# Attention and mixer on one core: loads of pairs 1 and 3, bursts of pairs 4 to 7, and new unit orders

## The chip, the cores and the metric

The kernel runs on one core of a Trainium2 chip. The metric is device time in microseconds of one execution; the time given is the median of several runs. Engines are TensorE (PE), VectorE (DVE), ScalarE (ACT), GpSimd (POOL) and SyncE (SP). SP, ACT and POOL issue DMAs; POOL's are software DMAs, which can also turn fp32 into bf16.

## The reference

```python
batch, n_heads, seq, head_dim = (4, 8, 768, 64); n_sink, window = (4, 128)
scores = scale * q @ k.T                      # scale = 1/sqrt(64)
keep = (key < n_sink) | (0 <= query - key < window)
a = softmax(where(keep, scores, -1e9)); attn = a @ v
x = attn as [4, 768, 512]                     # heads side by side
h = relu(x.T @ w_tok1) @ w_tok2               # w_tok1 768x256, w_tok2 256x768
u = x + h.T
out = u + relu(u @ w_ch1) @ w_ch2             # w_ch1 512x1536, w_ch2 1536x512
```

All inputs and the output are fp32.

## The kernel before

The 32 heads are worked on as 16 pairs, four (NHP) for each batch; pair p is batch p // 4. For a pair, q and k must come to lie with the head's 64 elements on the partitions (`qT`, `kT`); then come the scores of the window and of the sinks, exp, the mask, and the product with v (`v_aug`, with a column of ones for the sum of the weights).

**Loads.** Pairs 0 to 3: SP loads q and k as fp32 into a place each of `early` (`load_raw`), and an engine casts them to `q_bf`, `k_bf` (`cast`). Pairs 4 to 7: POOL's software DMA loads and casts; PE turns them. Pairs 8 to 15 (BY_DMA = 8): POOL's DMA loads and casts, and a DMA transpose of SP turns them. The v of all pairs and the four weights (T w_tok1, A w_tok2, C w_ch1 and D w_ch2 in quarters) are loaded by POOL. The four sink rows of v of batch 0's heads are loaded by SP in four DMAs into `v_sink_f`, and POOL casts that tile to `v_sink`. A cast waits for the landing, a turn for the cast.

**Turning by PE.** For pairs 0 to 4, `turn(p, n)` turns q (n = 0) or k (n = 1) into two of the four small PSUM banks (`mx`), 128x384 each. For pairs 5 to 7, `transposed(p)` turns q and k into one of the two double banks (`sc`), which two evictions of 128x768 read; since scores will later be written there by small tiles and then read whole, the bank's unwritten columns are set to zero (`cleared`, a memset of DVE).

**Scores.** `scores(p, g)` has three groups g of keys for a pair. `by_halves` makes four matmuls of 128 keys for a group (three in another shape for the last), `by_eighths` sixteen of 32 keys that leave out more of what the mask drops. Pairs 4 to 7 do group 0 by halves and the others by eighths; pairs 8 to 15 do all by eighths. `score_sinks(p)` makes the scores of the sinks of two pairs.

**Values.** `pv(p, half)` multiplies the weights with v and the sinks' weights with `v_sink`, in full tiles of 128 rows. Pairs 4 to 7 had another form: `sink_values(p)`, eight matmuls in small tiles within a burst, and two `values(p, i)`.

**Order.** A class `Plan` runs once, while the program is built. It holds a cost for each operation (`Op`) and a time for each landing (`landed(at)`), and gives each operation other than PE's to an engine and a place in its order. PE's order is given by tables: FIRST_BATCH for batch 0 (q0 and k0 turn pair 0's q and k; m01 adds the mask of pair 0's group 1 and s01 makes its scores; x1 makes the sinks' scores of pairs 0 and 1; o10 is `pv(1, 0)`; h0 the first step of the mixer over tokens; u00 and y01 the second step; t00 a transpose of u), MERGED for all that follows (t: units of `attention_and_tokens`; c: units of the mixer over channels, `mix_channels`), and LOADS for POOL's loads. A `burst` is one PE unit made of pieces that use small tiles (64 rows or 32 columns); PE changes between these and full tiles at its ends. `attention_and_tokens` makes two bursts for each of the pairs 4 to 7 and three for two pairs from 8 on.

Every engine runs its instructions in the order so fixed.

Of the kernel before, what the change touches and what calls it, by code (L numbers as in the profile page):

```python
# [9 lines left out]
FP32 = mybir.dt.float32  # L10
BF16 = mybir.dt.bfloat16
# [5 lines left out]
def kernel(  # L17
# [167 lines left out]
    raws = {p: load_raw(p) for p in range(2)}  # L185
    vs = {}


    ones = singles.tile([P, 4 * P], BF16)
    in_order(nc.vector.memset(ones, 1.0))  # L190

# [45 lines left out]
    v_sink_f = singles.tile([P, NHP, 2, D1], FP32)  # L237
    in_order(nc.vector.memset(v_sink_f, 0.0))
    for n in range(4):
        i, odd = n // 2, n % 2  # L240
        rows = slice(D * i + ODD * odd, D * i + ODD * odd + n_sink)
# [4 lines left out]
        in_order(nc.vector.memset(v_sink_f[rows, odd::2, i, D:D1], 1.0))  # L246
    raws.update({p: load_raw(p) for p in range(2, NHP)})
# [212 lines left out]
    def prepare(p):  # L460
# [4 lines left out]
        parts = 2 if p <= NHP else 1  # L465
# [55 lines left out]
    def transposed(p):  # L521

        def run():
            ps = turned_bank(p)
            for n in range(2):
                turn_rows(p, n, [ps[:, x, n] for x in range(2)])
                tiles["ps_" + "qk"[n], p] = ps[:, :, n].rearrange("d x j p -> d x p j")

        then = [*done["qT", p], *done["kT", p]]
        then.append(cleared(p, then))  # L530
        return piece(
            350, run, [done["q_bf", p], done["k_bf", p]], {"sc": [then]}, then, [("tq", p), ("tk", p)],
        )
# [37 lines left out]
    def scores(p, g):  # L571
# [4 lines left out]
        eighths = p >= BY_DMA or p >= NHP and g > 0  # L576
# [361 lines left out]
    def attention_and_tokens():  # L938
# [13 lines left out]
        for p in range(first, BY_DMA):  # L952
            b, hp = pairs[p]
            pieces = []
            prepare(p + 1)
            if p + 1 < BY_DMA:
                pieces.append(transposed(p + 1))
# [7 lines left out]
            if hp == NHP - 1:  # L965
                pieces += turned
            if hp % 2 == 0:
                pieces.append(score_sinks(p + 1))
            units.append(burst(*pieces))
            units[-1].then.append(sink_rows(p))  # L970
            if hp == 2:
                turned = tokens(b, 0)

        for p in range(BY_DMA, last, 2):
            b, hp = pairs[p]
            prepare(p + 1)
            units.append(burst(scores(p, 0), scores(p, 1)))
            units[-1].then.append(sink_rows(p))
            units += [pv(p - 1, half) for half in range(2)]
            turned = [] if hp else tokens(b - 1, 1)  # L980
            if p + 2 <= last:
                prepare(p + 2)
            units.append(burst(scores(p, 2), scores(p + 1, 0), score_sinks(p + 1), *turned))
            units[-1].then.append(sink_rows(p + 1))
            if hp == 0:
                parts.append(units)
                units = []
            units += [pv(p, half) for half in range(2)]
            if hp == 2:
                assert not tokens(b, 0)  # L990
            units.append(burst(scores(p + 1, 1), scores(p + 1, 2)))
# [318 lines left out]
    def cast(p, n, at):  # L1310
        cost = {"POOL": 850.0} if p == NHP - 1 else {"DVE": 570.0} if p or n else {"ACT": 850.0}
        return Op(cost, lambda e: copy(e, bf_tile(p, n), raws[p][n]), [landed(at)])

    for p, at in enumerate(((3900.0, 5300.0), (7500.0, 8600.0), (11300.0, 12500.0), (13500.0, 14700.0))):
        for n, name in enumerate(("q_bf", "k_bf")):
            queue((name, p), cast(p, n, at[n]))
    v_sink = Op({"POOL": 650.0}, lambda e: copy(e, v_sink0, v_sink_f), [landed(9000.0)])
# [3 lines left out]
    done["v", 0] = landed(12600.0)  # L1321
# [78 lines left out]
```

## Time and profile before

| | us |
|---|---|
| median of 3 runs | 195.93 (195.38 to 196.03) |
| profiled execution, time | 196.29 |
| profiled execution, span of the core | 194.5 |
| PE busy in the span | 186.1 (96%) |
| DVE, ACT, POOL busy | 135.0, 106.0, 60.2 |

The span runs from the first to the last recorded instruction; 1.8 us of the profiled execution lie around it. Busy time is that in which an instruction of the engine runs; the granted clock of PE is 1.0 throughout.

### The profile page before, as it was taken

How to read it: one execution, taken by the hardware profiler on the slowest of the kernel's cores; microseconds unless marked ns; L12 is line 12 of the kernel's file. 1: busy time of each engine (PE TensorE's matmuls, PEld its weight loads, DVE VectorE, ACT ScalarE, POOL GpSimd, SP SyncE). 2: the span in 40 equal slices, each digit the busy share in tenths (PEclk: the TensorE clock that was granted, in tenths of full speed). 3: DMA queues.
4: the chain of work that ended last, by engine and by line, in shares of the span. 5: the costliest groups of instructions: out<-in, count | busy, mean ns of one | idle time of the engine just before them, and what ended most of it. 6: DMA issues, size and time to landing. Idle time of an engine off the chain costs nothing.

```text
span 194.5 us, 5919 instructions
## 1 busy us (share of the span) xinstructions
PE 186.1 (96%) x2548; PEld 130.4 (67%) x2555; DVE 135.0 (69%) x299; ACT 106.0 (54%) x183; POOL 60.2 (31%) x78
## 2 busy tenths in 40 slices
PE   6896999999999999999999999999999999999992
PEld 1344797566664565566767887667668886667891
DVE  4678677887977657777789788786597762067671
ACT  4699747888864414777753536786461005764100
POOL 7379662509984851536900000000000000000000
PEclk9999999999999999999999999999999999999999
DMA  5999999999999999999999954500000717000036
GB/s 188 279 289 178 202 205 189 191 192 169 158 137 143 127 217 131 223 206 126 139 147 143 144 111 136 219 3 0 3 0 2 149 54 285 3 0 0 0 113 216
DMA packets 82139, 26.35 MB, mean 135 GB/s; under 512 B 69952, under 2 KB 79296, under 8 KB 82112
## 3 DMA queue, kind: packets, MB, share of 16 engines
q0 software_dynamic: 56864, 11.80, 75.7%
q1 hardware_dynamic: 25248, 14.17, 34.3%
q8 instruction: 20, 0.33, 0.7%
q14 instruction: 7, 0.06, 0.1%
HBM read 26.75 MB, written 6.29 MB: 170 GB/s over the span
## 4 chain that ended last, share of the span: by engine, by line
PE 87%; DMA 7%; DVE 2%; POOL 1%; issue 1%; SPq 0%; ACT 0%
PE ps_mx L163 76%; PE ps_sc L163 8%; DMA early<-in_q_dram 7%; DVE kT L172 1%; PE ps_sc L495 1%; PE ps_mx L166 1%; PE ps_mx L495 1%; SPq L124 0%; POOL k_bf L172 0%; POOL q_bf L172 0%; ACT qT L170 0%; POOL w_tok L181 0%; DVE o_sb L1107 0%; DVE pT L619 0%; DVE v1T L178 0%
## 5 line engine op out<-in xcount | busy, mean ns | idle before, releaser
L163 PE MATMUL ps_mx<-uT,w_ch 128*128 128x384 bf16 x384 | 69.5, 326 | 0.0
L176 ACT ACTIVATE v1T<-ps_mx 128x384 bf16<-128x384 f32 x81 | 39.8, 491 | 40.7 <-PE ps_mx L163 40.2
L611 ACT ACTIVATE pT<-ps_sc 128x1024 bf16<-128x1024 f32 (+1 forms) x48 | 44.3, 955 | 22.4 <-PE ps_sc L163 22.2
L163 PEld LDWEIGHTS <-w_ch 128*128 128x128 bf16 x384 | 35.6, 98 | 21.9 <-issue 0.9
L163 PE MATMUL ps_mx<-w_ch,v1T 128*128 128x256 bf16 (+1 forms) x164 | 29.1, 317 | 0.3 <-issue 0.2
L163 PEld LDWEIGHTS <-v1T 128*128 128x128 bf16 x234 | 22.5, 98 | 9.6 <-issue 0.2
L163 PEld LDWEIGHTS <-early 128*128 128x128 bf16 x222 | 21.3, 98 | 2.9
L163 PEld LDWEIGHTS <-w_tok 128*128 128x128 bf16 x240 | 19.7, 98 | 3.8 <-DVE x_sb L682 0.2
L156 POOL DMA_DIRECT2D v_aug<-in_v_dram x16 | 16.5, 1035 | 10.9 <-PE ps_mx L163 6.5
L828 DVE TENSOR_TENSOR u_sb<-ps_mx,x_sb 128x512 bf16<-128x512 f32 (+1 forms) x24 | 15.4, 655 | 5.5 <-PE ps_mx L163 5.3
L1262 DVE TENSOR_TENSOR early<-v1T 128x1152 bf16<-128x1152 bf16 x12 | 8.7, 754 | 12.6 <-ACT v1T L176 12.6
L163 PE MATMUL ps_mx<-v_aug,pT 128*128 128x65 bf16 x352 | 17.5, 193 | 0.0
L163 PEld LDWEIGHTS <-pT 128*128 128x128 bf16 x352 | 15.7, 97 | 2.6 <-issue 0.6
L147 POOL DMA_DIRECT2D k_bf<-in_k_dram x16 | 13.2, 835 | 10.1 <-DMA q_bf<-in_q_dram 4.8
L163 PE MATMUL ps_mx<-w_sums,early 128*128 128x256 bf16 x126 | 16.2, 273 | 0.0
L619 DVE TENSOR_TENSOR pT<-pT,mask_main 128x768 bf16<-128x768 bf16 (+1 forms) x25 | 15.0, 615 | 1.0 <-ACT pT L611 0.9
L1107 DVE TENSOR_TENSOR o_sb<-ps_mx,u_sb 128x256 f32<-128x256 f32 x28 | 11.7, 422 | 4.9 <-PE ps_mx L163 4.9
L147 POOL DMA_DIRECT2D q_bf<-in_q_dram x16 | 13.2, 840 | 5.8 <-DMA v_aug<-in_v_dram 4.9
L682 DVE TENSOR_TENSOR x_sb<-ps_mx,recip 128x384 bf16<-128x384 f32 x26 | 14.3, 555 | 0.8
L163 PE MATMUL ps_mx<-h1T,w_tok 128*128 128x256 bf16 (+1 forms) x120 | 14.2, 251 | 0.0
L163 PE MATMUL ps_sc<-qT,kT 64*32 64x160 bf16 (+7 forms) x576 | 13.7, 233 | 0.3 <-DVE ps_sc L544 0.2
L163 PEld LDWEIGHTS <-kT 64*32 64x32 bf16 (+1 forms) x608 | 7.3, 91 | 8.9 <-issue 7.6
(83 smaller groups left out, 206.2 us busy)
## 6 DMA issues: line engine op xcount, KB each, us to landing
out_dram<-o_sb SPq DMA_DIRECT2D x22, 256.0 KB, 2.6
v_aug<-in_v_dram POOLq DMA_DIRECT2D x16, 192.0 KB, 10.1
w_ch<-in_moe_w_ch_dram POOLq DMA_DIRECT2D x8, 384.0 KB, 10.8
early<-in_q_dram SPq DMA_DIRECT2D x4, 384.0 KB, 6.0
early<-in_k_dram SPq DMA_DIRECT2D x4, 384.0 KB, 6.8
q_bf<-in_q_dram POOLq DMA_DIRECT2D x16, 96.0 KB, 11.6
k_bf<-in_k_dram POOLq DMA_DIRECT2D x16, 96.0 KB, 9.5
k_bf<-in_k_dram POOLq DMA_DIRECT2D x4, 192.0 KB, 10.2
```

The source lines that it names most:

```text
L147: in_order(nc.gpsimd.dma_start(out=out[:, h], in_=rows[:, h]))
L156: in_order(nc.gpsimd.dma_start(out=v_aug.rearrange("p i t d -> p (i t) d")[:, :, 0:D], in_=v[b].rearrange("h s d -> (h s) d")[2 * hp * S:2 ...
L163: in_order(nc.tensor.matmul(*args, skip_group_check=True, **kwargs))
L166: in_order(nc.tensor.transpose(out, in_, ident))
L176: in_order(nc.scalar.activation(out, in_, AF.Relu))
L495: in_order(nc.tensor.transpose(outs[x][columns], block, ident[rows, rows]))
L611: in_order(nc.scalar.activation(part(tiles["pT", p][:, :, ds(2 * g, 2)]), of_keys(tiles["ps_s", p, g])[:, :, 0:width(g)], AF.Exp, scale=scale,
L619: in_order(nc.vector.tensor_tensor(out=pt, in0=pt, in1=m, op=ALU.mult))
L682: in_order(nc.vector.tensor_tensor(out=x_sb[b][:, ts(half, QH), ts(hp, 2 * D)].rearrange("p t (i d) -> p t i d", i=2), in0=tiles["ps_o", p ...
L828: in_order(nc.vector.tensor_tensor(out=u_part(b, g, s0, n), in0=tiles["ps_u", b, g, s0], in1=x_sb[b][:, s0:s0 + n, c0:c0 + cn], op=ALU.add,))
L1107: in_order(nc.vector.tensor_tensor(out=o_sb, in0=ps, in1=u_rows(b, st)[:, g, cols] if first else o_sb, op=ALU.add,))
L1262: lambda e, n=n, x=x, y=y, how=how: in_order(nc.vector.tensor_tensor(out=v1_sums[:, n, ds(j, SUMMED)], in0=of(x), in1=of(y), op=how,)), deps,
```

## The change

1. `load_raw`: pair 1's q and k are issued on ACT's queue, behind the load of its function table and an exp of one element (`first_act`). Pair 3's go into pair 1's places in `early`; their loads, issued by SP, wait for the casts of pair 1.
2. The sink rows come by one DMA onto four partitions, and four small copies put them into `v_sink` (`place_sinks`; the planner may choose ACT or DVE). The zeros and ones are now set in `v_sink` itself.
3. Pair 0's q is cast on DVE; pair 3's may be cast on POOL or DVE.
4. `transposed` takes two `mx` banks, each with q and k of one of the pair's two heads, and is followed by four evictions of 128x384; the memset goes.
5. Pairs 4 to 7 use the loop of the pairs from 8 on: three bursts for two pairs, group 0 by eighths, `pv` for the values of pairs 4 to 6.
6. Planner's numbers and all three tables are new.

```diff
     MERGED = (
-        "t1 t0 c13 t2 c16 c6 c9 t3 c8 c18 c3 t7 c10 c21 c12 c19 t4 c20 t6 t5 c23 c4 c17 t8 c14 t9 c15 t10 c1 c0 t11 c5 "
...
+        "t1 t0 t2 c20 t3 c17 c13 c16 c9 c18 t6 c12 c14 c23 c19 c21 t8 t7 c8 c3 t9 c5 c7 t5 c10 c2 t4 t10 c0 c6 t13 c1 "
...
     FIRST_BATCH = (
-        "q0 k0 m00 s00 m01 s01 q1 m02 k1 s02 m11 x1 s11 m10 q2 s10 o01 m12 k2 s12 o00 m21 q3 s21 s20 k3 o11 s22 x3 o10 "
-        "m31 s30 s31 o20 h0 m32 o21 s32 h1 o30 o31 y01 u00 h2 u10 u11 t00 h3 u20 t01 t11 y30 t10 u21 t20 t30 u31 t31 "
-        "t21"
+        "q0 k0 m02 s02 m01 s01 m00 q1 s00 k1 x1 m10 s10 q2 m11 k2 s11 o01 m12 s12 k3 o00 s22 o10 q3 s20 o11 m21 s21 x3 "
+        "h0 s30 m31 s31 o21 o20 h1 m32 u00 s32 u10 y01 u11 o30 t00 o31 h2 u21 h3 t01 u20 y30 t10 u31 t20 t30 t21 t31 "
+        "t11"
     )
...
-    def load_raw(pidx):
+    def load_raw(pidx, which=(0, 1)):
         raw = []
-        for n in range(2):
-            f = early[:, 2 * pidx + n]
-            in_order(nc.sync.dma_start(out=f, in_=rows_of(pidx, n).rearrange("p h j d -> p h (j d)")))
+        for n in which:
+            f = early[:, 2 * (1 if pidx == NHP - 1 else pidx) + n]
+            queue = nc.scalar if pidx == 1 else nc.sync
+            in_order(queue.dma_start(out=f, in_=rows_of(pidx, n).rearrange("p h j d -> p h (j d)")))
...
-    v_sink_f = singles.tile([P, NHP, 2, D1], FP32)
-    in_order(nc.vector.memset(v_sink_f, 0.0))
-    for n in range(4):
...
-        in_order(nc.sync.dma_start(
-            out=v_sink_f[rows, odd::2, i, 0:D],
-            in_=v[0].rearrange("(p o i) s d -> i o s p d", i=2, o=2)[i, odd, 0:n_sink],
-        ))
+    v_sink_f = singles.tile([n_sink, NHP, 2, D], FP32)
+    in_order(nc.sync.dma_start(
+        out=v_sink_f.rearrange("s p i d -> s (p i) d"), in_=v[0].rearrange("h s d -> s h d")[0:n_sink],
+    ))
...
         def run():
-            ps = turned_bank(p)
-            for n in range(2):
-                turn_rows(p, n, [ps[:, x, n] for x in range(2)])
-                tiles["ps_" + "qk"[n], p] = ps[:, :, n].rearrange("d x j p -> d x p j")
+            ps = [bank("mx", 2, NT, D, dtype=BF16) for _ in range(2)]
+            for n, name in enumerate("qk"):
+                tiles["ps_" + name, p] = [t[:, n].rearrange("d j p -> d p j") for t in ps]
+                turn_rows(p, n, [t[:, n] for t in ps])
...
-        eighths = p >= BY_DMA or p >= NHP and g > 0
+        eighths = p >= NHP
...
-        for p in range(first, BY_DMA):
...
-            pieces.append(scores(p, 0))
-            if p > first:
-                pieces.append(sink_values(p - 1))
-            units.append(burst(*pieces))
-            if p > first:
-                units += [values(p - 1, i) for i in range(2)]
-            pieces = [scores(p, 1), scores(p, 2)]
...
+        for p in range(first, last, 2):
...
+            units.append(burst(*ready(p + 1), scores(p, 0), scores(p, 1)))
...
+                units += [pv(p - 1, half) for half in range(2)]
...
+            units.append(burst(*ready(p + 2), scores(p, 2), scores(p + 1, 0), score_sinks(p + 1), *turned))
...
+            units += [pv(p, half) for half in range(2)]
+            turned = tokens(b, 0) if hp == 2 else []
+            units.append(burst(scores(p + 1, 1), scores(p + 1, 2), *turned))
...
     def cast(p, n, at):
-        cost = {"POOL": 850.0} if p == NHP - 1 else {"DVE": 570.0} if p or n else {"ACT": 850.0}
+        cost = {"POOL": 850.0, "DVE": 570.0} if p == NHP - 1 else {"DVE": 570.0}
...
+    def load_late(n):
...
+        queue(("raw", n), Op({"SP": 450.0}, load, [("qk"[n] + "_bf", 1)], lag=3300.0))
...
-    v_sink = Op({"POOL": 650.0}, lambda e: copy(e, v_sink0, v_sink_f), [landed(9000.0)])
+    def place_sinks(e):
+        for rows, odd, i in sink_places:
+            copy(e, v_sink0[rows, odd::2, i, 0:D], v_sink_f[:, odd::2, i])
+
+    v_sink = Op({"ACT": 800.0, "DVE": 800.0}, place_sinks, [landed(6200.0)])
```

What the planner makes of it is seen in the engines' orders. ACT at the start of the program before (the numbers behind a tile's name are buffers; `ps_mx_164` and `ps_mx_165` hold pair 0's q, `ps_mx_186` and `ps_mx_187` its k):

```order
L170 ACT_TABLE_LOAD
L170 ACTIVATE q_bf_160<-early_75 128x2x6x64
L170 ACTIVATE qT0_129<-ps_mx_164 128x384
L170 ACTIVATE qT0_129<-ps_mx_165 128x384
L170 ACTIVATE kT0_125<-ps_mx_186 128x384
L170 ACTIVATE kT0_125<-ps_mx_187 128x384
L611 ACTIVATE pT0_133<-ps_sc0_73 128x2x512
```

And now (`early` from `in_q_dram` and `in_k_dram` are pair 1's loads):

```order
L192 ACT_TABLE_LOAD
L192 ACTIVATE first_act_87<-ones_85 1x1
L125 DMA early_75<-in_q_dram 128x2x384
L125 DMA early_75<-in_k_dram 128x2x384
L171 ACTIVATE qT0_135<-ps_mx_159 128x384
L171 ACTIVATE kT0_131<-ps_mx_177 128x384
L171 ACTIVATE kT0_131<-ps_mx_178 128x384
L171 ACTIVATE v_sink_144<-v_sink_f_91 4x2x64 x4
L614 ACTIVATE pT0_139<-ps_sc0_73 128x2x384
```

The cast of pair 0's q and one of its evictions left ACT, two DMA issues and the four sink copies came ahead of the first exp.

POOL before, from its first load on (`k_bf_162` is pair 4's k; `q_bf_338` and `k_bf_384` are pair 3's):

```order
L156 DMA v_aug0_77<-in_v_dram 128x12x64
L142 DMA k_bf_162<-in_k_dram 128x2x384
L172 CAST v_sink_138<-v_sink_f_139 128x520
L156 DMA v_aug1_78<-in_v_dram 128x12x64
L156 DMA v_aug2_79<-in_v_dram 128x12x64
L181 DMA w_tok1_154<-in_moe_w_tok1_dram 128x6x256
L156 DMA v_aug3_80<-in_v_dram 128x12x64
L172 CAST q_bf_338<-early_75 128x2x6x64
L181 DMA w_tok2_155<-in_moe_w_tok2_dram 128x2x768
L172 CAST k_bf_384<-early_75 128x2x6x64
```

And now (`k_bf_259` and `q_bf_265` are pair 4's, `k_bf_339` is pair 3's):

```order
L157 DMA v_aug0_77<-in_v_dram 128x12x64
L157 DMA v_aug1_78<-in_v_dram 128x12x64
L182 DMA w_tok1_151<-in_moe_w_tok1_dram 128x6x256
L143 DMA k_bf_259<-in_k_dram 128x2x384
L143 DMA q_bf_265<-in_q_dram 128x2x384
L157 DMA v_aug2_79<-in_v_dram 128x12x64
L182 DMA w_tok2_152<-in_moe_w_tok2_dram 128x2x768
L173 CAST k_bf_339<-early_75 128x2x6x64
L157 DMA v_aug3_80<-in_v_dram 128x12x64
```

The sinks' cast and that of pair 3's q left POOL; seven loads stand ahead of the cast of pair 3's k, pair 4's q among them, which came later before.

DVE in the program's start before, behind the turns of pair 2 and 3 (`ps_mx_364` is pair 3's q, `ps_mx_392` pair 4's k, `ps_mx_422` and `ps_mx_423` pair 3's k; L679 and L682 are the end of `pv`):

```order
L172 COPY kT2_127<-ps_mx_323 128x384
L679 RECIPROCAL recip_377<-ps_mx_345 128x6
L682 TENSOR_TENSOR x_sb0_158<-ps_mx_345,recip_377 128x3x128
L172 COPY qT3_132<-ps_mx_364 128x384
L172 COPY kT0_125<-ps_mx_392 128x384
L172 COPY kT3_128<-ps_mx_422 128x384
L172 COPY kT3_128<-ps_mx_423 128x384
L619 TENSOR_TENSOR pT2_135<-pT2_135,mask_first_98 128x2x512
```

And now (`k_bf_273` is pair 2's k, `q_bf_283` pair 3's q, `ps_mx_354` pair 3's k):

```order
L173 CAST k_bf_273<-early_75 128x2x6x64
L173 CAST q_bf_283<-early_75 128x2x6x64
L173 COPY qT2_137<-ps_mx_285 128x384
L173 COPY qT2_137<-ps_mx_286 128x384
L173 COPY kT2_133<-ps_mx_305 128x384
L682 RECIPROCAL recip_347<-ps_mx_323 128x6
L685 TENSOR_TENSOR x_sb0_155<-ps_mx_323,recip_347 128x3x128
L173 COPY kT3_134<-ps_mx_354 128x384
L682 RECIPROCAL recip_388<-ps_mx_368 128x6
```

Pair 3's k is evicted right behind the first `pv` and ahead of its q, its q is cast here, and one of the two evictions of its k went to ACT.

More of the change, by code (lines that the diff above doesn't have):

```diff
@@ L184 @@
     tiles = {}
-    raws = {p: load_raw(p) for p in range(2)}
+    raws = {0: load_raw(0)}
     vs = {}
@@ L464, in prepare @@
         kT = kTb[p % NKB]
-        parts = 2 if p <= NHP else 1
+        parts = 2
         def evict(e, n, part):
@@ L523, in run @@
         def run():
-            ps = turned_bank(p)
-            for n in range(2):
-                turn_rows(p, n, [ps[:, x, n] for x in range(2)])
-                tiles["ps_" + "qk"[n], p] = ps[:, :, n].rearrange("d x j p -> d x p j")
+            ps = [bank("mx", 2, NT, D, dtype=BF16) for _ in range(2)]
+            for n, name in enumerate("qk"):
+                tiles["ps_" + name, p] = [t[:, n].rearrange("d j p -> d p j") for t in ps]
+                turn_rows(p, n, [t[:, n] for t in ps])
         then = [*done["qT", p], *done["kT", p]]
-        then.append(cleared(p, then))
         return piece(
-            350, run, [done["q_bf", p], done["k_bf", p]], {"sc": [then]}, then, [("tq", p), ("tk", p)],
+            350, run, [done["q_bf", p], done["k_bf", p]], {"mx": [[done[x, p][part] for x in ("qT", "kT")] for part in range(2)]},
+            then, [("tq", p), ("tk", p)],
         )
@@ L950, in tokens, with ready @@
             return [turned_u(b, g)]
-        for p in range(first, BY_DMA):
+        for p in range(first, last, 2):
             b, hp = pairs[p]
[L954 to L957, printed above, removed]
-            pieces.append(scores(p, 0))
-            if p > first:
-                pieces.append(sink_values(p - 1))
-            units.append(burst(*pieces))
-            if p > first:
-                units += [values(p - 1, i) for i in range(2)]
-            pieces = [scores(p, 1), scores(p, 2)]
[L965 to L983, printed above, removed]
+            def ready(n):
+                if n <= last:
+                    prepare(n)
+                return [transposed(n)] if n < BY_DMA else []
+            units.append(burst(*ready(p + 1), scores(p, 0), scores(p, 1)))
+            units[-1].then.append(sink_rows(p))
+            turned = []
+            if p > first:
+                units += [pv(p - 1, half) for half in range(2)]
+                if hp == 0:
+                    turned = tokens(b - 1, 1)
+            units.append(burst(*ready(p + 2), scores(p, 2), scores(p + 1, 0), score_sinks(p + 1), *turned))
             units[-1].then.append(sink_rows(p + 1))
-            if hp == 0:
+            if hp == 0 and p > first:
                 parts.append(units)
@@ L1301 @@
     plan = Plan()
-    plan.free.update(PE=3000.0, ACT=2200.0, DVE=3900.0, POOL=4100.0)
-    plan.queue = 13000.0
-    plan.landings.append(12500.0)
+    plan.free.update(PE=3000.0, ACT=2200.0, DVE=3900.0, POOL=4600.0)
+    plan.queue = 12500.0
+    plan.landings.append(11200.0)
     def queue(key, op):
@@ L1320 @@
     plan.pending.append(v_sink)
-    done["v", 0] = landed(12600.0)
+    done["v", 0] = landed(11500.0)
     for name in LOADS.split():
```

33 lines of the change are left out of this document (19 added, 14 removed), and 18 rows, old and new, of the table MERGED.

## The prediction

> **What bounds the kernel now.** I read the page's busy times first, then windows of 2 us over the start, then the chain of waits that ended last, and at the end the timeline around each row that the change moves. The page:
>
> ```profile
> span 194.5 us, 5919 instructions
> ...
> PE 186.1 (96%) x2548; PEld 130.4 (67%) x2555; DVE 135.0 (69%) x299; ACT 106.0 (54%) x183; POOL 60.2 (31%) x78
> ```
>
> TensorE (PE) has work for 96% of the span. A change can then win in two ways only: fill the few holes of PE, or give PE less to do. The windows (from:to, then PE, PEld, DVE, ACT and POOL busy with counts, PE clock, DMA share, GB/s) show where the holes are; the last three are cut to the stretches that the argument below needs:
>
> ```profile
> 12.00:14.00 2.00, 2.00 (x41) 1.05 (x42) 1.39 (x4) 2.00 (x4) 1.22 (x2) 1.00 1.34 338
> 14.00:16.00 2.00, 1.69 (x48) 1.17 (x49) 1.84 (x5) 1.86 (x4) 1.45 (x2) 1.00 2.33 167
> 16.00:18.00 2.00, 1.62 (x57) 1.26 (x55) 1.67 (x4) 2.00 (x3) 2.00 (x4) 1.00 1.63 192
> 18.00:20.00 2.00, 1.14 (x20) 0.57 (x17) 1.97 (x6) 1.69 (x4) 2.00 (x4) 1.00 1.95 180
> ...
> 14.42:16.91 2.49, 1.80 (x59) 1.18 (x59) 2.09 (x6) 2.35 (x5) 2.36 (x4) 1.00 2.14 178
> 16.91:23.13 6.22, 5.21 (x99) 3.80 (x101) 5.17 (x13) 5.13 (x8) 5.01 (x7) 1.00 1.53 193
> 19.09:190.30 171.21, 170.55 (x2325) 123.28 (x2331) 121.82 (x261) 91.51 (x162) 47.09 (x56) 1.00 1.10 122
> ```
>
> From 14 to 20 us PE is idle for 0.31, 0.38 and 0.86, together 1.55 us. From 19.09 to 190.3 it is idle for 0.66 us in all. So after 20 us only a smaller amount of PE work can make the kernel faster. The chain (start, length, engine or DMA, tile, line) names what made the early holes:
>
> ```profile
> 7.94 6.55 DMA early<-in_q_dram
> 14.55 0.82 POOL q_bf L172
> ...
> 16.02 0.84 POOL k_bf L172
> 16.91 0.39 PE ps_mx L504 x12
> ...
> 19.09 0.86 PE ps_mx L163 x15
> ```
>
> Pair 3's q was issued at 7.94, landed at 14.5, and POOL cast it; POOL then issued a weight load, cast pair 3's k at 16.02, and only at 16.91 could PE turn that k (the unit k3). What follows hangs on it.
>
> **The start.** PE runs its units in order, so what stands behind k3 waits for k3. Before, the units o00 m21 q3 s21 s20 and pair 4's k fill 14.42 to 16.91, the units from k3 to s32 fill 16.91 to 23.13. PE's work in them is 1.80 and 5.21 us (last windows but one). In the new order nearly all of the first group, and h1, u00 and pair 4's q too, stand between k3 and the end of s32. These last three are priced from start to start in PE's timeline:
>
> ```profile
> 23.13 0.84 PE L163 MATMUL ps_mx<-x_sb,w_tok 128*128 128x128 bf16 x12
> 23.81 0.35 PE L163 MATMUL ps_mx<-v_aug,pT 128*128 128x65 bf16 x6
> ...
> 29.07 0.50 PE L163 MATMUL ps_mx<-h1T,w_tok 128*128 128x128 bf16 x6
> 29.40 0.59 PE L166 MATMUL ps_mx<-ident,u_sb 128*128 128x128 bf16 x6
> ...
> 30.25 0.43 PE L495 MATMUL ps_mx<-ident,q_bf 64*64 64x64 bf16 x24
> 30.62 0.82 PE L163 MATMUL ps_mx<-uT,w_ch 128*128 128x384 bf16 x4
> ```
>
> h1 is 0.68, u00 0.33, pair 4's q 0.37: 1.4 us. From the start of k3's turn to the end of s32 PE then has 1.80 + 5.21 + 1.4 = 8.4 us of work. Before, s32 ended at 23.13 and those 1.4 us still lay ahead, so the same work was done at 24.5. If PE is dense behind k3, the gain is 24.5 − 8.4 − t = 16.1 − t, where t is the start of k3's turn. Each microsecond by which k3 is later than 16.1 costs one; each that it is earlier brings one. The order allows it no earlier than about 14.5: ahead of k3 now stand 134 matmuls, before 191, and of those 59 lie in the window from 14.42 to 16.91, so that 132 were done at 14.42. The term lies between −1.6 and an open end on the other side.
>
> When does k3 start? It needs pair 3's k landed, then POOL's cast (0.84, the chain's row at 16.02) and 0.05 for the hand-over. Landing is the unknown. These rows bear on it (timeline, then a DMA issue with KB and median us to landing):
>
> ```profile
> 7.95 0.56 DVE L172 CAST q_bf<-early 128x768 bf16<-128x768 f32 x1 [1.37 <-DMA early<-in_q_dram]
> 8.70 0.61 POOL L172 CAST v_sink<-v_sink_f 128x520 bf16<-128x520 f32 x1 [3.30 <-DMA v_sink_f<-in_v_dram]
> 9.01 0.72 DVE L172 CAST k_bf<-early 128x768 bf16<-128x768 f32 x1 [0.50 <-DMA early<-in_k_dram]
> ```
>
> ```profile
> v_aug<-in_v_dram POOLq DMA_DIRECT2D x16, 192.0 KB, 10.1
> ```
>
> Pair 3 now has to wait until pair 1's casts have emptied its place (8.5 and 9.7 in this trace), so its issue hardly moves: from 7.94 to about 8.6 for q, to about 9.8 for k. But pair 2 goes out sooner, as no four sink loads stand ahead of it, and pair 1 has a queue of its own, so behind SP's issue of pair 3 only pair 2 is in the ring. Against that, POOL no longer waits 3.30 us for the sink rows and sends v0, v1, w_tok1, k4, q4, v2 and w_tok2 without a break. In this trace the software queue's loads were slow beside the others: 10.1 us for 192 KB. They seem to give way, but they also took the rate down: 338 GB/s at 12 to 14, 167 at 14 to 16. From q3's 6.55 us a k issued at 9.8 would land at 16.3 if nothing changed; with the ring empty ahead of it, in the time of one load between two of this trace (7.95 to 9.01, 1.1 us) plus some latency, by 13. I take 14.5, the place where pair 3's q lands today. Then t = 14.5 + 0.9 = 15.4, and the gain is 0.7.
>
> Pair 3's q sets a second bound. DVE now casts it ahead of both evictions of pair 2's q, and o01, which stands ahead of k3, needs a bank that these free. Before, o01 to the end of s12 took 1.4 us, the turn of pair 2's k among them; without that some 1.2:
>
> ```profile
> 12.96 0.23 PE L163 MATMUL ps_mx<-v_sink,pT_sink 128*128 128x130 bf16 x1
> ...
> 14.37 0.35 PE L163 MATMUL ps_mx<-v_aug,pT 128*128 128x65 bf16 x6
> ```
>
> With q landed at L, cast (0.6) and one eviction (0.5) put o01 at L + 1.1 and k3 at L + 2.3. For t = 15.4 L is 13.1; q goes out 1.2 us ahead of k, so it would be there at 13.3 if k is there at 14.5: the two bounds are level. Landing as today at 14.5 it would put k3 at 16.8.
>
> **Weighed against that.** The trace's row at 12 to 14 shows 338 GB/s with loads of two issuers in flight, and less right after, not more. [...]
>
> **What lies beside.** Two casts of about 0.6 us (7.95) move to DVE from ACT and POOL, and some evictions of q and k in the start change engines. DVE is at 1.84, 1.67 and 1.97 of each 2 us there; POOL's 0.61 for the sinks becomes four ACT copies of a few rows ahead of the first exp. One of these may hold PE for 0.1 to 0.3. I take 0.1, so the start gives −0.6.
>
> **Pairs 4 to 7.** From here PE is dense, so start-to-start times are prices:
>
> ```profile
> 41.19 0.39 PE L163 MATMUL ps_sc<-qT,kT 64*128 64x256 bf16 x4
> 41.42 0.28 PE L163 MATMUL ps_mx<-v_sink,pT_sink 64*128 64x65 bf16 x8
> 41.63 0.82 PE L163 MATMUL ps_mx<-uT,w_ch 128*128 128x384 bf16 x4
> ...
> 49.58 0.44 PE L163 MATMUL ps_sc<-qT,kT 64*32 64x160 bf16 x32
> 49.85 0.40 PE L163 MATMUL ps_mx<-qT,kT 64*32 64x512 bf16 x4
> ...
> 82.34 0.22 PE L163 MATMUL ps_mx<-v_sink,pT_sink 128*128 128x130 bf16 x1
> 82.40 0.29 PE L163 MATMUL ps_mx<-v_aug,pT 128*128 128x65 bf16 x4
> ...
> 83.26 0.49 PE L163 MATMUL ps_sc<-qT,kT 64*32 64x256 bf16 x32
> 83.69 0.50 PE L163 MATMUL ps_mx<-uT,w_ch 128*128 128x384 bf16 x2
> ```
>
> - Group 0 by eighths: two groups, 32 matmuls, took 0.27 (49.58 to 49.85), so 0.13 each, against 0.23 by halves (41.19 to 41.42). Four groups: −0.4, though 48 matmuls are added.
> - Two bursts fewer: the same 32 matmuls took 0.43 where full tiles follow (83.26 to 83.69), so leaving a burst costs 0.16. −0.3.
> - Sinks of pairs 4 to 6: 8 small matmuls at 0.21 (41.42 to 41.63), of which 0.16 is the leaving that is paid anyway, become four at 0.06 (82.34 to 82.40). 0.24 − 0.05 = +0.19, three times: +0.6 at most; if the leaving was hidden there, +0.1. I take +0.4.
> - No cleared bank: PE's one wait on it goes, −0.2 (waits of PE: tile, line, releaser, us, count, longest):
>
> ```profile
> PE ps_sc L163 <- DVE ps_sc L544: 0.2, 1, 0.2
> ```
>
> - Evictions (by form, busy and mean ns). For pairs 5 to 7 one of each wide kind becomes two of each narrow kind:
>
> ```profile
> L170 ACT ACTIVATE qT<-ps_sc 128x768 bf16<-128x768 bf16 x3 | 2.4, 812 | 0.5 <-PE ps_sc L495 0.4
> L172 DVE COPY kT<-ps_sc 128x768 bf16<-128x768 bf16 x3 | 2.9, 958 | 2.7 <-ACT qT L170 2.7
> L544 DVE MEMSET ps_sc<- 64x384 f32 x3 | 1.1, 378 | 0.4
> ...
> L170 ACT ACTIVATE qT<-ps_mx 128x384 bf16<-128x384 bf16 x6 | 2.9, 495 | 1.2 <-PE ps_mx L504 0.6 <-PE ps_mx L495 0.5
> ```
>
> 0.81 + 0.96 + 0.38 = 2.15 us per pair become 4 of about 0.5, on engines that PE has not waited for after 20 us but once, so nothing on the path. What could be late instead is the mx banks: a turned pair now holds two of the four for its evictions, and the channel products, which need one for every group of their matmuls, could stand still. Before, no such wait is seen; bounds 0 and +0.3 per pair, I take 0, as other work of PE lies between.
>
> Sum here: −0.4 − 0.3 + 0.4 − 0.2 = −0.5; I take −0.4, as the switch was priced at one place. Bounds −0.9 and +0.5 (all three pairs wait for banks).
>
> **The rest.** Pairs 8 to 15 are computed as before in another order, and the output's last stores are ordered anew. With 0.66 us of idle from 19 to 190 there is nothing to win; a misplaced unit could cost. 0, within ±0.5.
>
> **The sum.** The profiled execution took 196.29 (span 194.5 and 1.8 around it). 196.29 − 0.6 − 0.4 = 195.3. The median of the runs, 195.93, is 0.36 below that execution, so the forecast is **194.9**. No change is 195.3 to 196.5 (0.3%, 0.59 us, about what a measurement of this kernel can tell from none).
>
> **Rivals.**
>
> A, slower, 0.28: the loads that POOL now sends early take the DMA engines from pair 3, and PE stands at k3 with 8.4 us of work behind it that could have run. For it: the rate fell to half when software loads joined; pair 3's issue waits for two casts. Against: software loads were the slow ones. It decides from a landing of k at 15.6 (of q at 14.2), where −0.4 is eaten; from 16.2 (14.8) it is slower by over 0.3%. With k at 17.0 k3 starts at 17.9, +1.8, which with −0.4 gives 195.93 + 1.4 = 197.3.
>
> B, no change, 0.12: pair 3 lands when it did, t is near 16.1, the start gives 0, and a wait for mx banks takes back part of the 0.4. 195.5 to 195.9; I say 195.7. This also holds the case that the change doesn't do what it says, since the issue of pair 3 hardly moves.
>
> C, more, 0.20: pair 3's k lands by 13.7, t is 14.5 to 14.7, and the start gives 1.4 to 1.6; with the 0.4 that is 195.93 − 2.0 = 193.9, and down to 193.5 where the sinks cost less. For it: PE stands ready that early. Against: DVE and ACT, both over eight tenths busy there, would have to keep up.
>
> **How the numbers follow.** The forecast's own case has 0.40, of which 0.05 lies within 0.3%. Faster: 0.35 + 0.20 = 0.55; same: 0.05 + 0.12 = 0.17; slower: 0.28. The range 193.5 to 197.2 takes in C and A up to a landing at 16.9. The likeliest case's own range is 194.4 to 195.4.
>
> **What would show it.** Right: DVE's cast of pair 3's q starts at about 13, POOL's of its k at 14 to 15, PE's turn of it at about 15.4, s32 ends about 23.8 with h1, u00 and pair 4's turn done; PE's idle from 14 to 20 is under 1 us; the groups of eighths in pairs 4 to 7 take 0.13; idle after 20 us stays at 0.7. Wrong: PE waits over 1 us for POOL's cast ahead of k3, or for DVE's eviction ahead of o01 (A); s32's end beyond 24.5; new waits of PE on evictions of q or k after 30 us (the banks); or a row of this trace's kind, such as the exp or the loads of v, ending the idle time ahead of the values.

## The result, and the profile after

The changed kernel takes 205.66 us (median of 4 runs, 204.99 to 207.46) against 195.9: a ratio of 1.052, with a 95% interval of 1.045 to 1.059. The forecast was 194.9, in a range up to 197.2. Here and below, medians are of all runs of a kernel, and ratios leave out runs that are over 1.5% above its fastest. The profiled execution took 204.99, its span is 203.2, 8.7 longer than before. The page after:

```profile
span 203.2 us, 6003 instructions
PE 190.2 (94%) x2591; PEld 132.4 (65%) x2591; DVE 136.9 (67%) x301; ACT 107.2 (53%) x190; POOL 59.1 (29%) x76
```

PE is busy 4.1 us longer and idle 4.6 us longer. What PE waited for (tile, line, releaser: us in all, times, longest):

```profile
PE ps_mx L507 <- POOL k_bf L173: 1.8, 1, 1.8
...
PE ps_mx L164 <- DVE qT L173: 1.4, 1, 1.4
PE ps_mx L164 <- issue: 1.4, 1, 1.4
PE ps_sc L164 <- DVE o_sb L1093: 1.0, 2, 0.5
PE ps_sc L164 <- issue: 1.0, 1, 1.0
```

There are three places: the start (POOL's k_bf, DVE's qT), two waits on "issue", for which the profile shows no releaser, and the end (o_sb). Rows of the timeline at the start:

```profile
8.35 0.37 SPq L125 DMA_DIRECT2D early<-in_q_dram  x1
9.73 0.37 SPq L125 DMA_DIRECT2D early<-in_k_dram  x1
15.40 0.56 DVE L173 CAST q_bf<-early 128x768 bf16<-128x768 f32 x1 [2.49 <-DMA early<-in_q_dram]
16.48 0.22 PE L164 MATMUL ps_mx<-v_sink,pT_sink 128*128 128x130 bf16 x1 [1.44 <-DVE qT L173]
18.67 0.82 POOL L173 CAST k_bf<-early 128x768 bf16<-128x768 f32 x1 [8.82 <-DMA early<-in_k_dram]
19.54 0.47 PE L507 MATMUL ps_mx<-ident,k_bf 64*128 64x64 bf16 x12 [1.78 <-POOL k_bf L173]
29.53 0.34 PE L164 MATMUL ps_sc<-qT,kT 64*128 64x256 bf16 x4
```

Pair 3's loads went out when the forecast said, at 8.35 and 9.73. But q landed at 15.4 instead of 13.3, k at 18.6 instead of 14.5. The late q held DVE with pair 2's evictions behind it, and o01 on PE; the late k held PE again. The DMA queues from 9.5 to 12 us (packets, MB, share of 16 engines), after and then before:

```profile
q0 software_dynamic: 2616, 0.40, 220.4%
q1 hardware_dynamic: 13, 0.02, 2.1%
```

```profile
q0 software_dynamic: 666, 0.23, 78.8%
q1 hardware_dynamic: 318, 0.46, 55.8%
```

Before, SP's packets flow beside the software ones. Now, with pair 3's two loads issued, SP's queue gets 13 packets through in these 2.5 us, while POOL's loads, issued from 3.55 us on, get 2616. And PE's clock falls, seen in windows of 2 us after:

```profile
18.00:20.00 2.00, 0.46 (x14) 0.37 (x14) 0.04 (x1) 0.62 (x1) 1.33 (x2) 0.90 1.87 186
20.00:22.00 2.00, 2.00 (x32) 1.51 (x32) 1.31 (x3) 1.23 (x2) 2.00 (x4) 0.50 1.10 139
22.00:24.00 2.00, 2.00 (x35) 1.17 (x37) 1.55 (x5) 1.61 (x4) 2.00 (x3) 0.74 1.74 147
```

After two waits of 1.44 and 1.78 us within 5 us, with 1.3 us of work between them (16.48 to 17.77), PE has a granted clock of 0.50: 0.62 from 19.5 to 20 us, 0.50 from 20 to 23, 0.97 from 23 to 23.5. How much idle time is needed stays open: below, a single wait of 2.11 us is followed by half clock too (`e5_warm`), and one of 2.21 us is not (`e3_own_place`).

The account of the 8.7 us, from the rows and the experiments below. Its parts are places in the span, not prices: what was saved at one was partly lost at the next.

| | us |
|---|---|
| pair 3 late: k3's turn 3.56 later than with pair 3 early, half clock behind it 1.37 | 4.9 |
| the new start even with pair 3 early | 0.3 |
| two waits on issue, at 34 and 41 us | 2.4 |
| two waits for sc banks at the end | 1.0 |
| all else, pairs 4 to 7 among it | 0.1 |

### The profile page after: what moved, and what is told of

It is laid out like the page before. It is cut to its first block, busy times and chain, and to the rows that moved or that the text cites. A ratio compares the mean times of both kernels' runs of the same rounds, so it can differ in the third digit from the quotient of the medians.

```text
span 203.2 us, 6003 instructions
## 1 busy us (share of the span) xinstructions
PE 190.2 (94%) x2591; PEld 132.4 (65%) x2591; DVE 136.9 (67%) x301; ACT 107.2 (53%) x190; POOL 59.1 (29%) x76
## 4 chain that ended last, share of the span: by engine, by line
PE 87%; DMA 8%; issue 1%; DVE 1%; ACT 1%; POOL 0%
PE ps_mx L164 75%; PE ps_sc L164 9%; DMA early<-in_k_dram 8%; PE ps_mx L498 2%; PE ps_mx L167 1%; DVE o_sb L1093 1%; ACT L192 1%; PE ps_mx L507 0%; POOL k_bf L173 0%; DVE k_bf L173 0%
## 5 line engine op out<-in xcount | busy, mean ns | idle before, releaser
L177 ACT ACTIVATE v1T<-ps_mx 128x384 bf16<-128x384 f32 x82 | 40.3, 491 | 42.8 <-PE ps_mx L164 41.4
L164 PEld LDWEIGHTS <-w_ch 128*128 128x128 bf16 x384 | 36.1, 98 | 21.7 <-issue 1.0
L164 PE MATMUL ps_mx<-w_ch,v1T 128*128 128x256 bf16 (+1 forms) x168 | 30.0, 319 | 0.0
L164 PEld LDWEIGHTS <-pT 128*128 128x128 bf16 x352 | 17.0, 100 | 3.9 <-issue 1.4
L831 DVE TENSOR_TENSOR u_sb<-ps_mx,x_sb 128x512 bf16<-128x512 f32 (+1 forms) x24 | 15.4, 654 | 6.2 <-PE ps_mx L164 6.1
L164 PE MATMUL ps_mx<-v_aug,pT 128*128 128x65 bf16 x352 | 18.7, 196 | 0.0
L685 DVE TENSOR_TENSOR x_sb<-ps_mx,recip 128x384 bf16<-128x384 f32 x32 | 17.3, 552 | 0.8
L164 PE MATMUL ps_mx<-w_sums,early 128*128 128x256 bf16 x126 | 15.4, 273 | 0.0
L164 PE MATMUL ps_sc<-qT,kT 64*32 64x160 bf16 (+6 forms) x624 | 14.2, 235 | 1.2 <-issue 1.0
L148 POOL DMA_DIRECT2D q_bf<-in_q_dram x16 | 13.3, 848 | 6.4 <-DMA v_aug<-in_v_dram 2.5
L164 PE MATMUL ps_mx<-v_sink,pT_sink 128*128 128x130 bf16 x64 | 12.9, 224 | 1.4 <-DVE qT L173 1.4
L148 POOL DMA_DIRECT2D k_bf<-in_k_dram x16 | 13.3, 846 | 1.6 <-DVE pT L622 0.7
```

What stands on the lines that cost most here:

```text
L148: in_order(nc.gpsimd.dma_start(out=out[:, h], in_=rows[:, h]))
L164: in_order(nc.tensor.matmul(*args, skip_group_check=True, **kwargs))
L177: in_order(nc.scalar.activation(out, in_, AF.Relu))
L685: in_order(nc.vector.tensor_tensor(out=x_sb[b][:, ts(half, QH), ts(hp, 2 * D)].rearrange("p t (i d) -> p t i d", i=2), in0=tiles["ps_o", p ...
L831: in_order(nc.vector.tensor_tensor(out=u_part(b, g, s0, n), in0=tiles["ps_u", b, g, s0], in1=x_sb[b][:, s0:s0 + n, c0:c0 + cn], op=ALU.add,))
```

## The experiments

**Whose fault: the start or pairs 4 to 7?** Two hybrids. `e1_old_start` is the kernel before with only the new code of pairs 4 to 7 and the new MERGED:

```diff
-        eighths = p >= BY_DMA or p >= NHP and g > 0
+        eighths = p >= NHP          # and the loop, transposed(), MERGED of after
```

> Edit: the kernel before, with only the part on pairs 4 to 7 of the change (one loop, eighths, turning into mx banks) and the new MERGED; loads, sinks, casts, FIRST_BATCH and LOADS as before. Theory 1 (of the 8.7 us that the span of the changed kernel is longer, about 5.3 arise before the end of s32 and the rest are PE's two waits on issue at 34 and 41 us, 2.4, and two waits for sc banks at the end, 1.0): the start's 5.3 go, so 199 to 201.5 with the waits still there. Rival (the late start sets the later waits off as well): 195.5 to 197. Second rival (pairs 4 to 7 themselves cost the most): 203 or more.

`e2_old_mid` is the changed kernel with the old code of pairs 4 to 7 and the old MERGED.

> Edit: the changed kernel with pairs 4 to 7 and MERGED as before; loads, sinks, casts, FIRST_BATCH and LOADS stay changed. Theory 1: the start's 5.3 us stay, pair 3's k is cast at 18.5 or later and PE is at half clock from 19.5 to 23; the waits on issue and on sc banks go or shrink: 200.5 to 202.5. Rival (waits on issue follow from the late start): as long as the changed kernel, 204 to 206.

Measured: 210.84 (ratio 1.078, 1.074 to 1.082) and 204.53 (1.047, 1.041 to 1.053). The first is slower than both its parents. Its time is what the second rival allows, but not for that rival's reason, as PE's waits are new ones:

```profile
PE ps_mx L163 <- DMA w_ch<-in_moe_w_ch_dram: 3.8, 2, 2.9
PE ps_mx L163 <- DVE v_sink L172: 3.1, 1, 3.1
PE ps_mx L163 <- ACT v_sink L170: 2.9, 1, 2.9
```

The old LOADS does not bring what the new MERGED wants next (`v_sink` is copied from v, and ACT waited 7.55 us for a v ahead of one such copy). So this hybrid does not price pairs 4 to 7. The second keeps the late start (1.7 and 1.6 us of waits on pair 3's k and q) and loses the sc waits, which so belong to the new MERGED; its waits on issue shrink from 2.4 to 0.6. Yet its 204.5 lies above the expected 200.5 to 202.5: it has new waits of 0.5 on h1T and kT, and its clock is 0.50 in every window from 18 to 24 us, longer than in the changed kernel.

**Pair 3 in a place of its own.** `e3_own_place` leaves every order as it is and takes only the wait away:

```diff
-            f = early[:, 2 * (1 if pidx == NHP - 1 else pidx) + n]
+            f = early[:, 2 * pidx + n]
-    raws[NHP - 1] = [None, None]
+    raws[NHP - 1] = load_raw(NHP - 1)
```

> Edit: the changed kernel, but pair 3 is loaded into a place of its own, issued by SP right behind pair 2, with no wait for the casts of pair 1; all other orders are the same. Theory 1 (pair 3's loads came late since their issue waited, the ring ran empty and the software packets of v0, v1 and w_tok1 went first): its q lands by 12.5, its k by 14.5, PE turns k before 16, no half clock: 199 to 201. Rival (the 16 DMA engines are simply full, whoever issues): k still lands after 17 and the time stays above 203.

Measured: 200.75 (1.024, 1.019 to 1.030). Theory 1 holds. The queues from 9.5 to 12 us, and rows of its timeline:

```profile
q1 hardware_dynamic: 459, 0.66, 85.3%
q0 software_dynamic: 594, 0.08, 46.4%
```

```profile
13.10 0.95 POOL L173 CAST k_bf<-early 128x768 bf16<-128x768 f32 x1 [3.31 <-DMA early<-in_k_dram]
15.98 0.34 PE L507 MATMUL ps_mx<-ident,k_bf 64*128 64x64 bf16 x12
24.60 0.34 PE L164 MATMUL ps_sc<-qT,kT 64*128 64x256 bf16 x4
31.36 0.33 PE L164 MATMUL ps_mx<-h1T,w_tok 128*128 128x128 bf16 x3 [2.21 <-issue]
37.83 0.32 PE L164 MATMUL ps_sc<-qT,kT 64*32 64x160 bf16 x13 [1.02 <-issue]
```

Pair 3's k is there at 13.1, and s32 starts 4.93 us sooner than in the changed kernel (24.60 against 29.53). It ends at 24.9, where the work before stood at 24.5: the new start, freed of its fault, gains nothing. Of the 4.9 us the span gets only 3.5, since the first wait on issue grows from 1.43 to 2.21 and another follows at 52.

**The same loads without POOL's.** `e10_held` keeps pair 3's wait, and holds POOL back after v0:

```diff
-    done["v", 1].deps.append(v_sink)
+    done["v", 1].deps += [v_sink, ("k_bf", NHP - 1)]
```

> Edit: the changed kernel, but POOL issues nothing after v0 until it has cast pair 3's k; pair 3's loads still wait for pair 1's casts. Theory 1 (pair 3's k came at 18.6 because v1, w_tok1 and pair 4 fill the DMA engines while its own issue waits): with v0 alone beside it pair 3's k lands by 15; what POOL issues after that comes late, so the whole time says little, 203 to 210. Rival (the wait for the casts alone makes it late): k lands at 17.5 or later all the same.

Measured: 204.73. The time says little, as expected, but the landing does:

```profile
13.24 1.01 POOL L173 CAST k_bf<-early 128x768 bf16<-128x768 f32 x1 [8.55 <-DMA early<-in_k_dram]
```

Issued as late as in the changed kernel, at 9.37, the k landed at 13.2 instead of 18.6, 3.8 us after its issue instead of 8.9. So the wait alone does not make it late; the software loads that overtake it do.

**The half clock.** `e5_warm` fills the second wait with idle matmuls:

```diff
+            if (p, n) == (NHP - 1, 1):
+                keep_warm(8, given["mx"][0])
```

> Edit: the changed kernel with 8 idle matmuls of 512 columns on PE ahead of the turn of pair 3's k, where PE waits 1.8 us anyway. Theory 1 (the idle time of 3.2 us between 15 and 19.5 puts PE at half clock for 3.4 us, worth 1.6 us): clock stays at 1.0, 1.3 to 1.7 us faster than the changed kernel, about 204.1. Rival (the half clock comes anyway or costs nothing, as PE waits for others there): same time within 0.4 us.

Measured: 205.04 (1.047, 1.044 to 1.050), 0.6 below the changed kernel and within its spread: no gain to speak of, yet the rival's reason fell. Rows of k3 and s32, a window, and the first wait on issue:

```profile
19.11 0.35 PE L507 MATMUL ps_mx<-ident,k_bf 64*128 64x64 bf16 x12
...
27.74 0.34 PE L164 MATMUL ps_sc<-qT,kT 64*128 64x256 bf16 x4
...
20.00:22.00 2.00, 2.00 (x48) 1.35 (x44) 1.93 (x7) 1.76 (x5) 2.00 (x4) 1.00 1.55 177
...
34.13 0.25 PE L164 MATMUL ps_sc<-qT,kT 64*32 64x160 bf16 x4 [2.11 <-issue]
```

The clock stayed at 1.00 here, and from k3's turn to s32 PE took 8.63 us (19.11 to 27.74) instead of 9.99 (19.54 to 29.53): the half clock had cost 1.4. s32 came 1.8 us sooner, 0.4 of it because pair 3's k was cast sooner in this run (18.19 against 18.67). But at the first wait on issue PE then stood 2.11 instead of 1.43, and a second spell of half clock followed (0.63 from 34 to 36 us, 0.51 from 36 to 38). What was saved at one wait was lost at the next.

**What is "issue"?** Windows from 0 to the middle of each wait count PE's matmuls so far (each has a weight load, so two instructions). The changed kernel, then the one with own places:

```profile
0.00:33.90 33.90, 27.95 (x478) 15.99 (x479) 22.31 (x58) 21.42 (x36) 20.61 (x32) 0.95 1.30 212
0.00:41.00 41.00, 33.53 (x606) 20.31 (x607) 27.33 (x71) 25.73 (x43) 25.15 (x37) 0.96 1.40 206
```

```profile
0.00:29.00 29.00, 26.28 (x478) 15.10 (x479) 22.57 (x58) 20.91 (x36) 18.67 (x29) 1.00 1.33 224
0.00:36.70 36.70, 31.73 (x606) 19.40 (x607) 27.41 (x70) 25.05 (x43) 23.57 (x35) 1.00 1.42 215
0.00:52.40 52.40, 46.41 (x862) 28.88 (x862) 39.66 (x99) 36.37 (x63) 32.13 (x45) 1.00 1.52 202
```

478, 606, 862: the steps are 128 and 256 matmuls, 256 and 512 instructions. `e8_own_phase` moves every later instruction by 98:

```diff
-    keep_warm(7, 0)               # 7 matmuls of 512 columns
+    keep_warm_narrow(56, 0, 64)   # 56 of 64, on top of own places
```

> Edit: the changed kernel with pair 3 in its own place, and the 7 warm-up matmuls of 512 columns cut into 56 of 64 columns, so that every later PE instruction has a number higher by 98. Theory 1 (PE's instructions come in blocks of 256 and a block takes 4.7 to 6.5 us to come, so PE waits where a block ends, whatever stands there): the waits on issue are again behind PE's instructions number 955, 1211 or another multiple of 256 from these, and so at other matmuls than without the shift. Rival (these waits belong to a certain matmul, by an unseen dependency): they stay at the same matmuls, now 1053 and 1309.

Measured: 199.36 (1.018, 1.014 to 1.022), with waits in these places:

```profile
0.00:28.80 28.80, 25.88 (x478) 16.65 (x479) 21.48 (x57) 20.34 (x34) 18.34 (x29) 1.00 1.33 222
0.00:34.80 34.80, 31.60 (x606) 21.17 (x607) 26.28 (x70) 24.59 (x42) 22.05 (x33) 1.00 1.38 217
0.00:47.20 47.20, 43.53 (x862) 28.76 (x862) 36.05 (x92) 34.75 (x61) 30.10 (x43) 1.00 1.44 210
```

```profile
29.10 0.31 PE L503 MATMUL ps_mx<-ident,k_bf 64*64 64x64 bf16 x14 [0.24 <-issue]
...
35.30 0.25 PE L503 MATMUL ps_mx<-ident,q_bf 64*64 64x64 bf16 x6 [0.47 <-issue]
...
47.54 0.82 PE L164 MATMUL ps_mx<-uT,w_ch 128*128 128x384 bf16 x4 [0.23 <-issue]
```

The same counts, other matmuls, and 0.9 us of waits instead of 3.6. The DMA queues of the changed kernel's profile show the loads of instructions themselves. The whole span, then the windows 33.2 to 33.3 and 39.6 to 39.7 (packets, MB, share):

```profile
q8 instruction: 20, 0.33, 0.7%
```

```profile
q8 instruction: 1, 0.02, 59.3%
```

```profile
q8 instruction: 1, 0.02, 59.0%
```

PE's 2 times 2591 instructions are 20.2 times 256, and the queue moves 20 packets of 16.5 KB. PE goes on at 35.51 and 41.98, 2.2 to 2.4 us after the two packets; with own places packets at 28.9, 35.5 and 50.3 stand 2.3 to 2.6 us ahead of 31.36, 37.83 and 52.86, where its three waits end. So PE's instructions come in blocks of 256 in these runs (256 and 512 from wait to wait), and PE waits when it gets through a block before the next is there: 1.43 and 1.02 us in the changed kernel, 2.21 and 1.02 at the first two places with own places. Why the kernel before waited on issue for only 0.2 us, two windows over the same instructions, the block that ends at the 478th matmul, show (before, then after):

```profile
26.05:31.89 5.84, 5.84 (x130) 5.25 (x131) 4.47 (x11) 3.63 (x8) 2.92 (x4) 1.00 1.33 202
```

```profile
30.76:33.86 3.10, 3.10 (x130) 2.82 (x128) 2.40 (x7) 1.79 (x5) 1.48 (x2) 1.00 1.44 199
```

130 matmuls in 5.84 us or in 3.10: the new orders put turns, eighths and pv in a row where channel products, slow and few, stood between. The next block came 4.75 us after the block's start (30.76 to 35.51), the one behind it 6.47 us later (41.98), in the kernel with own places 5.5 after the block's start.

`e9_probe` is the kernel before with 640 idle matmuls of 64 columns at two places (239.22 us, one run).

> Edit: the kernel before with 640 idle matmuls of 64 columns (1280 PE instructions) in one go at two places of the channel mixing, the first of batch 0, where POOL's loads keep the DMA engines busy, the second of batch 2, with no loads left. Theory 1: at both places PE stops every 256 instructions; in the first a block takes 4.7 to 6.5 us. If DMA traffic makes it slow, a block of the second place takes 2 to 3 us; rival: the same 5 to 6.5 us there. Second rival (blocks don't bind): PE runs all 1280 without a stop, in 10 to 18 us each.

PE's timeline at the first and at the second place:

```profile
37.12 3.96 PE L163 MATMUL ps_mx<-ones 128*128 128x64 bf16 x130
42.74 3.91 PE L163 MATMUL ps_mx<-ones 128*128 128x64 bf16 x128 [1.66 <-issue]
48.66 12.86 PE L163 MATMUL ps_mx<-ones 128*128 128x64 bf16 x382 [2.01 <-issue]
...
146.83 19.52 PE L163 MATMUL ps_mx<-ones 128*128 128x64 bf16 x640
```

Among the loads a block of 128 matmuls took 5.9 us (42.74 to 48.66), 2.0 of them waiting. Behind 48.66 three blocks follow without a wait, and by then the loads are through: the DMA share is 1.09 from 44 to 46 us and 0.04 from 48 to 50. At the second place (share 0.06 from 150 to 160) 128 took 3.9 on average (19.52 for 640), with no wait worth a row; the stops that theory 1 expected there did not come. So DMA traffic makes the blocks late; how fast they come without it stays open, as PE itself needs 3.9.

**Can the parts be had together?** `e6_own_old_mid` (own places, old pairs 4 to 7 and MERGED) and `e7_own_old_mid_warm` (the same and two idle matmuls ahead of pair 0's turns):

```diff
+            if p == 0:
+                keep_warm(1, given["mx"][0])
```

> Edit: the changed start, but with pair 3 in a place of its own and issued at once; pairs 4 to 7 and MERGED as before. Theory 1 (with pair 3 early the new start is 0.3 us behind the old one at the end of s32, 24.87 against 24.5; the waits on issue and the end's sc waits belong to the new MERGED): 195.5 to 197. Rival (the new FIRST_BATCH itself packs PE's instructions too densely, so waits on issue stay): 198 or more.

> Edit: the kernel above, and one more idle matmul of 512 columns on PE ahead of each of the turns of pair 0's q and k, where PE waits 0.5 us each. Theory 1 (PE's first matmuls run at half speed until 12.4 us, since it is idle twice between 4.6 and 6.2; without the holes it is at full speed about 3 us sooner, and nothing else waits there): 1.0 to 1.6 us faster than the kernel above. Rival (full speed comes at the same time, or the loads bound the start): same within 0.4 us.

Measured: 203.91 (201.16 to 208.07) and 203.71. The first expectation failed by 7 us: PE waited 4.1 us for a quarter of w_ch, which the new LOADS sends later than the old MERGED wants it. The idle matmuls brought 0.2, and the two profiles show why they can't be judged: PE's first matmuls ran at full rate in both, with and without them (pair 0's q turned in 0.35 us), while in the changed kernel they ran at half rate until about 12.4 us (0.50 for the same turn; the mask's two matmuls of 512 columns took 1.04 at 9.60 and 0.60 at 12.89) and in the kernel before until about 9.6. In the probe, whose start is that of the kernel before, pair 0's k turned in 0.35 too. So this rate differs between executions of the same start (0.50 and 0.35 for the same turn), also where the column of the granted clock says 1.00 throughout.

`e11_own_one_queue` puts pair 1 on SP's queue (own places kept):

```diff
-            queue = nc.scalar if pidx == 1 else nc.sync
+            queue = nc.sync
```

> Edit: the changed kernel with pair 3 in its own place at once, and pair 1 issued by SP ahead of the sinks and pair 2, no load on ACT's queue. [...]

Measured: 202.84 (201.27 to 203.98), 2.1 above the kernel with own places. Pair 3's k landed at 14.6 instead of 13.1; but PE was held earlier, by another wait:

```profile
9.68 1.28 ACT L171 ACTIVATE v_sink<-v_sink_f 4x128 bf16<-4x128 f32 x4 [2.28 <-DMA v_sink_f<-in_v_dram]
...
11.85 1.03 PE L164 MATMUL ps_sc<-mask_add,ident 128*128 128x512 bf16 x2 [2.98 <-ACT pT L614]
```

The sink rows now stood behind pair 1, the four copies behind them, the first exp behind those, and PE for 3 us behind that. So ACT's queue is not priced apart from the sinks.

`e13_own_phase_tail_warm` adds to the shifted kernel the old order of MERGED's last 24 units and the two idle matmuls.

> Edit: the changed kernel with pair 3 in its own place, the 56 narrow warm-up matmuls, the last 24 units of MERGED in the order that they had before, and one idle matmul of 512 columns ahead of each of the turns of pair 0. Theory 1: the two sc waits at the end go (1.0), PE is at full speed about 2 us sooner (1.0): 199.4 less 2.0 = 197.4. Rival (the idle matmuls bring nothing): 198.4. Either way not below the kernel before.

Measured: 198.25 (1.013, 1.011 to 1.016). The sc waits, 1.0 us, are gone. In this profile PE ran at full rate from pair 0's k on (0.35 at 6.31, its q 0.50 at 5.42; the mask's two of 512 columns took 0.60 at 7.87, in the shifted kernel 1.03 at 8.23), and s32 starts at 23.73 instead of the shifted kernel's 25.11, though PE now waited 0.8 and 0.5 for ACT's exp and kT. As `e6_own_old_mid` ran at full rate without idle matmuls, this isn't shown to be their work. The waits on issue grew from 0.9 to 1.3 us, and the span is 1.4 shorter in all (197.5 to 196.1), so the two parts are not priced apart. At full rate, too, the new start is not ahead: s32 ends at 24.00 here, and in the probe, which has the old start, at 22.27, with the 1.4 us of h1, u00 and pair 4's q still to come, 23.7.

`e14_before_sinks` is the kernel before with the change's sink rows alone.

```diff
-    v_sink = Op({"POOL": 650.0}, lambda e: copy(e, v_sink0, v_sink_f), [landed(9000.0)])
+    v_sink = Op({"ACT": 800.0, "DVE": 800.0}, place_sinks, [landed(9000.0)])
```

> Edit: the kernel before, with the sink rows by one DMA and four small copies in place of four DMAs and POOL's cast, and nothing else of the change. Theory 1 (the four sink loads took four of the eight places that let SP's later loads out only when earlier ones had landed, and held POOL for 3.3 us): pair 3's loads are issued by 5.5 us, its k lands by 14, PE's idle time from 14 to 20 shrinks by about 1: 194.4 to 195.2. Rival (POOL's loads, sent sooner, slow pair 3 by as much): 195.5 to 196.3.

Measured: 198.43 (1.015, 1.009 to 1.020), outside both. The loads did come sooner: POOL casts pair 3's q at 12.7 instead of 14.55 and its k at 14.5 instead of 16.0. But POOL's own issues changed places with them, and PE waited 0.8 for v and less for x_sb and exp. Nor does the run hold the sink rows alone: the planner put the four copies on DVE (in the change they are ACT's) and ordered other work of DVE and ACT anew. So the sinks are not priced by it. No kernel here beats the one before.

## Why the prediction was wrong

**The step that failed** is the landing of pair 3. The prediction had two arguments about it and chose the wrong one. "With the ring empty ahead of it" was counted as an advantage, and the software loads "seem to give way". The runs show the opposite: k was forecast for 14.5; it landed at 18.6 with its loads issued behind POOL's, at 13.1 issued early (own places), and at 13.2 issued late but with only POOL's v0 ahead. That is rival A, which had 0.28, with the places where PE stood, o01 and k3, as the prediction's two bounds have them.

A landing in time would not have brought the forecast gain either. With k at 13.1 (own places), sooner than the forecast's 14.5, k3 came at 15.98, not at 15.4 or at case C's 14.5 to 14.7, and s32 ended at 24.87 instead of 23.8. The prediction took k3's earliest time from a count, 134 matmuls against 132; the same count took PE about 1.5 us longer than in the kernel before. Part of this goes with the half rate of the first matmuls: where they ran at full rate (`e13_own_phase_tail_warm`), k3 came at 15.10.

**The size** was missed even by that rival. With k at 18.6 its rule gives t = 19.5 and 16.1 − 19.5 = −3.4 us, so about 199. The rule 8.4 + t nearly held without the clock: 8.9 in the kernel with own places (15.98 to 24.87) and in the kernel with idle matmuls (19.11 to 28.01). After the waits it was 10.3 (19.54 to 29.80, 0.27 behind s32's start), since PE fell to half clock: 1.4 us. The prediction had no term for what an idle PE costs afterwards.

**"The rest: 0, within ±0.5"** failed by 3.4: 2.4 us of instruction blocks and 1.0 of sc banks at the end. The prediction counted 48 added matmuls and two bursts fewer as PE time only. It read from 0.66 us of idle time that nothing could be won after 20 us, which no run contradicts, and gave a misplaced unit half a microsecond, which was too little.

**Pairs 4 to 7.** The waits feared on mx banks did not come: no eviction of q or k stands in the list of PE's waits after 20 us. Eighths took what the prediction said: two groups 0.28 us in the shifted kernel (35.66 to 35.94). But the gain of 0.4 is not to be seen, as the remainder of the account is 0.1; a kernel that had it alone could not be made, since `e1_old_start` met other waits. This term stays open within about half a microsecond.

## What to carry to other kernels

When a load is made to wait, ask what will have been queued by the time it goes out. Here the packets beside it, more than its issue time, set the landing of pair 3's k: issued at 9.73 us behind POOL's loads it took 8.9 us (SP's queue moved 13 packets from 9.5 to 12 us, the software queue 2616), issued at 9.37 with POOL's v0 alone ahead 3.8. Queued early, in a place of its own, it landed at 13.1, as 459 packets of SP's went through beside 594 software ones. In a kernel whose orders were fixed for one set of landings, tables and landings belong together: two of three hybrids that joined the new MERGED or LOADS with an old partner were slower than both their parents. The count of PE's instructions per microsecond is part of such an order: behind 256 in 3.1 us PE waited 1.43 us on issue, with about as many in 5.84 us its waits on issue were 0.2 in all.

## What the runs showed of the hardware

PE's waits on issue lay 256 of its instructions apart in the changed kernel, 256 and 512 in the kernel with own places; in the probe they came behind 130 and again behind 128 idle matmuls, each with a weight load. Among heavy loads a block of 256 took 4.75 to 6.47 us to come (4.75 and 6.47 in the changed kernel, 5.9 in the probe); 256 instructions in 3.1 us were too many, and in 5.84 not. A shift by 98 instructions took PE's waits on issue from 3.6 to 0.9 us. The waits ended 2.2 to 2.6 us after a packet of 16.5 KB on the instruction queue. Two waits of 1.44 and 1.78 us, with 1.3 us of work between them, were followed by a granted clock of 0.50 from 19.62 to 23.03 us, and one of 2.11 by 0.63 from 34 to 36 and 0.51 from 36 to 38; behind one of 2.21 it stayed at 1.00. PE's first matmuls ran at half rate in some profiles (pair 0's q turned in 0.50 us in the changed kernel) and at full rate in others (0.35 in `e6_own_old_mid`); s32 starts at 25.11 in a profile of the one kind and at 23.73 in one of the other. SP's hardware queue, with two loads newly issued, got 13 packets through in 2.5 us beside 2616 software packets.
